# A fused attention and two-layer MoE kernel on one core: its work buffers in two shared pools, the low halves of the softmax weights in two operations, and a new order

## The chip, the core and the metric

The kernel runs on one core of a Trainium2 chip. A core has TensorE (matmuls, PE in the rows, its weight loads PEld), VectorE (DVE), ScalarE (ACT), GpSimd (POOL) and SyncE (SP), which here issues all transfers. Each has a queue of its own and works through it in order. The metric is the time of one execution in microseconds on the device; lower is better.

## The reference

```python
def _attn_ref(q, k, v):            # q, k, v: 4 x 8 x 576 x 64
    scores = scale * np.matmul(q, k.transpose(0, 1, 3, 2))
    kth = np.partition(scores, -top_k, axis=-1)[..., -top_k:-top_k + 1]   # top_k = 32
    scores = np.where(scores >= kth, scores, -1000000000.0)
    scores = scores - np.max(scores, axis=-1, keepdims=True)
    attn = np.exp(scores)
    attn = attn / (np.sum(attn, axis=-1, keepdims=True) + 1e-09)
    return np.matmul(attn, v).astype(np.float32)

def _moe_ref(x, w_in, w_out):      # 2304 tokens, 512 -> 2048 -> 512
    h = x @ w_in
    g = h * (1.0 / (1.0 + np.exp(-1.702 * h)))
    return (g @ w_out).astype(np.float32)

def _moe2_ref(x, w1, w2, w3, w_out):   # 512 -> 1024 twice, product, 1024 -> 1024 -> 512
    return (((x @ w1) * (x @ w2) @ w3) @ w_out).astype(np.float32)
```

The output of the attention, as 2304 tokens of 512, goes through `_moe_ref` and then `_moe2_ref`.

## The kernel before

**Tiles.** The 2304 tokens are 18 tiles of 128. A tile has eight heads, so there are 144 heads of 128 rows and 576 columns; head 48, counted from 0, is the first of the seventh tile. A head goes like this: TensorE makes the scores in one of two score buffers `s_ps` (L997). VectorE finds the 32 largest of each row by four MAX8 (L1019) with a MATCH_REPLACE8 between them (L1022), which writes the scores without the eight just found to `wsb`. ScalarE cuts (L1037) and takes the exponential to `ysb` (L1040), which frees the score buffer. A high half in 16 bits is made of it (ScalarE L1046, GpSimd L1097 or VectorE L1094), then a low half, the rest that the high half misses: 64 columns (L1049) and 512 (L1050), on GpSimd. A DMA transposes both halves to `ats` (L1053), and TensorE multiplies them with the values (L1065).

**Products of two halves.** All large products are made of such pairs: high by high, high by low and low by high, three matmuls of 512 columns (L733 to L735). So the queries, keys, values and every intermediate result of the two MoE layers are scaled, rounded to a high half and have a low half taken from the rest. `split_op` does this for inputs (L404, L421 or L407 the high half; L414 on VectorE, or L417 or L424 with L418 or L427, the low half on GpSimd). The weights come as 64-bit numbers and are taken apart (L477 to L501) and split (L586 to L615) in the first 220 us, beside the first heads.

**The order.** Every step is recorded as an operation with a list of engines that could do it. `PLAN`, a packed table of numbers, gives each its rank and its engine, and `Order.run` issues the operations by rank. It also hands out buffers: a pool is a list of free slots, and an operation that acquires one gets the slot that came free first by the planner's own costs. On the chip the operation waits by semaphores for those that used the slot before it. So the table fixes the order of every engine and the neighbours in each buffer, and a wait in the queue of an engine holds up all that stands behind it.

**Buffers.** Each kind has its own pool: `w` 2 and `y` 3 of 2304 bytes a partition, `hl` 3 (the two halves of a head); `t` 4, `x2t` 1, `h` 3, `f` 3, `stg` 1 of 2 KB (transposed halves, halves, 32-bit intermediate results, loaded inputs).

Of the kernel before, what the change touches and what calls it, by code (L numbers as in the profile page):

```python
# [37 lines left out]
class Order:  # L38
# [17 lines left out]

    def op(self, alts, due, deps=(), env=None, acq=(), rel=(), tag="", lat=None, data=0.6, after=None):
# [4 lines left out]
        o.acq = [(a, env, a) if isinstance(a, str) else a for a in acq]  # L62
        o.rel = [(a, env, a) if isinstance(a, str) else a for a in rel]
# [5 lines left out]
    def run(self, log=None):  # L69
        free = dict.fromkeys("TVAGD", 0.0)  # L70
        lock = moved = 0.0
        for o in sorted(self.ops, key=lambda o: o.rank):
            e, cost, fn, _ = o.alts[0]
            if e == "N":
                o.eng = e
                o.start = o.end = max([0.0] + [d.end + self.GAP[d.eng] for d in o.deps])
                for name, env, key in o.acq:
                    env[key] = None
                continue
# [4 lines left out]
            for name, env, key in o.acq:  # L84
# [16 lines left out]
            for name, env, key in o.rel:  # L101
                if env[key] is not None:
                    self.pools[name].append((o.end + self.GAP[e], o.seq, env[key]))
# [51 lines left out]
    'Z88NeBX2;BpS<7}a;fA{9-3o4++sJJi+b6b8Y<qV-JH(E%6YN~fm6)sS8au^qu)A!uyVPCh?siYP2i?P!k5@k9o{jCN%u)s_GnARi0p*zTSb3>@QNH>8'
# [94 lines left out]
def kernel(  # L250
# [96 lines left out]
    def each(t, n):  # L347
        return [t[:, i] for i in range(n)]
# [1093 lines left out]
```

## Time and profile before

| | |
|---|---|
| median of 3 runs | 1024.83 us (1024.53 to 1025.07) |
| the profiled execution | 1027.73 us, its span 1026.0 us |
| mean granted clock of TensorE | 0.976 |
| TensorE busy, of the span | 947.2 us, 92% |
| VectorE busy | 925.1 us, 90% |
| GpSimd busy | 818.0 us, 80% |
| ScalarE busy | 793.9 us, 77% |

The span is from the first to the last instruction; the execution's own time has what lies around it. Matmuls overlap in time, so TensorE's busy share says that something was running, not that it ran at its peak. The engines have different limits at different times, so the shares are read by stretch of the span.

### The profile page before, as it was taken

The numbers are of one execution on the slowest core, as the hardware profiler recorded it, in microseconds if no ns is written. First come the engines' busy times: TensorE is split into PE (matmuls) and PEld (weight loads), VectorE is DVE, ScalarE is ACT, GpSimd is POOL, SyncE is SP. The second block draws the span as 40 slices with busy tenths as digits, with TensorE's granted clock in tenths as the row PEclk, the third lists the DMA queues.
The fourth block names the chain that finished last, engine by engine and source line by source line (L and its number), as shares of the span: only waits on it lengthen the run. The fifth ranks groups of instructions, "written<-read, shape, count | busy, mean of one in ns | idle before, by whom it ended". The sixth has DMA issues, their size and how long they took to land.

```text
span 1026.0 us, 18847 instructions
## 1 busy us (share of the span) xinstructions
PE 947.2 (92%) x5975; PEld 499.4 (49%) x5975; DVE 925.1 (90%) x2017; ACT 793.9 (77%) x1509; POOL 818.0 (80%) x1195
## 2 busy tenths in 40 slices
PE   4488987889999989999999999999999999999998
PEld 2255554444444544555545554555455545555543
DVE  4998998999999999999999999999999999998543
ACT  7887889977777878888988987878786887667432
POOL 3688788988889988998889998898788878768311
PEclk9689997999999999999999999999999999999999
DMA  8989777877586858688697786678667757545401
GB/s 271 273 274 333 252 171 172 181 160 115 104 140 111 156 98 166 132 144 151 122 164 137 132 160 128 125 130 163 122 130 132 140 103 128 107 89 111 83 1 42
DMA packets 401028, 150.09 MB, mean 146 GB/s; under 512 B 378912, under 2 KB 387104, under 8 KB 400928
## 3 DMA queue, kind: packets, MB, share of 16 engines
q1 hardware_dynamic: 400928, 148.89, 70.1%
q8 instruction: 47, 0.77, 0.3%
q14 instruction: 53, 0.43, 0.1%
HBM read 52.43 MB, written 4.72 MB: 56 GB/s over the span
## 4 chain that ended last, share of the span: by engine, by line
PE 45%; DVE 14%; POOL 13%; ACT 10%; DMA 7%; issue 4%; SPq 0%; POOLq 0%; ACTq 0%; DVEq 0%
PE mm L733 12%; PE mm L734 12%; PE mm L735 12%; DVE m8s L1019 6%; DVE wsb L1022 5%; PE s_ps L997 4%; PE mm L1065 3%; DMA tsb<-hsb 3%; POOL hlb L1050 2%; POOL fsb L1235 2%; DMA stg<-in_q_dram 2%; ACT ysb L1040 2%; POOL hsb L1197 1%; POOL hsb L418 1%; ACT s_ps L1037 1%
## 5 line engine op out<-in xcount | busy, mean ns | idle before, releaser
L1019 DVE MAX8 m8s<-wsb 128x8 f32<-128x576 f32 x432 | 322.3, 753 | 5.6
L1022 DVE MATCH_REPLACE8 wsb<-m8s,wsb 128x576 f32<-128x576 f32 x288 | 213.8, 742 | 0.0
L733 PE MATMUL mm<-w,tsb 128*128 128x512 f16 x432 | 164.5, 381 | 6.9 <-DMA tsb<-hsb 3.6
L735 PEld LDWEIGHTS <-tsb 128*128 128x128 f16 x1072 | 105.0, 98 | 129.3 <-issue 1.9
L733 PEld LDWEIGHTS <-tsb 128*128 128x128 f16 x1072 | 105.0, 98 | 125.4 <-DMA tsb<-hsb 11.5
L1050 POOL TENSOR_TENSOR hlb<-ysb,hlb 128x512 f16<-128x512 f32 x143 | 165.6, 1158 | 0.0
L734 PE MATMUL mm<-w,tsb 128*128 128x512 f16 x432 | 164.2, 380 | 0.0
L735 PE MATMUL mm<-w,tsb 128*128 128x512 f16 x432 | 164.0, 380 | 0.0
L734 PEld LDWEIGHTS <-tsb 128*128 128x128 f16 x1072 | 105.2, 98 | 113.2 <-issue 8.1
L1037 ACT ACTIVATE s_ps<-s_ps,m8s 128x576 f32<-128x576 f32 x144 | 102.4, 711 | 55.2 <-DVE m8s L1019 54.5
L733 PE MATMUL mm<-wout,tsb 128*128 128x512 f16 x344 | 130.8, 380 | 3.4 <-DVE wout L501 1.7
L1040 ACT ACTIVATE ysb<-s_ps,nbs,asm 128x576 f32<-128x576 f32 x144 | 119.8, 832 | 15.2 <-POOL nbs L1029 4.4
L735 PE MATMUL mm<-wout,tsb 128*128 128x512 f16 x344 | 130.6, 380 | 0.9 <-ACT tsb L678 0.9
L734 PE MATMUL mm<-wout,tsb 128*128 128x512 f16 x344 | 130.6, 380 | 0.0
L1019 DVE MAX8 m8s<-s_ps 128x8 f32<-128x576 f32 x144 | 108.9, 757 | 15.2 <-PE s_ps L997 11.2
L733 PE MATMUL mm<-win,tsb 128*128 128x512 f16 x296 | 113.0, 382 | 2.6 <-DMA tsb<-hsb 2.6
L735 PE MATMUL mm<-win,tsb 128*128 128x512 f16 x296 | 112.7, 381 | 0.0
L734 PE MATMUL mm<-win,tsb 128*128 128x512 f16 x296 | 112.7, 381 | 0.0
L997 PE MATMUL s_ps<-kts,qts 128*128 128x288 f16 (+1 forms) x640 | 97.8, 292 | 14.8 <-ACT ysb L1040 11.6
L1022 DVE MATCH_REPLACE8 wsb<-m8s,s_ps 128x576 f32<-128x576 f32 x144 | 107.6, 747 | 0.0
L1235 POOL TENSOR_TENSOR fsb<-fsb 128x512 f32<-128x512 f32 x68 | 86.9, 1278 | 7.7 <-ACT fsb L1232 4.8
L1197 POOL TENSOR_TENSOR hsb<-fsb,hsb 128x512 f16<-128x512 f32 x68 | 78.8, 1158 | 16.5 <-ACT hsb L1191 11.8
(309 smaller groups left out, 1849.9 us busy)
## 6 DMA issues: line engine op xcount, KB each, us to landing
w<-in_moe_w_out_dram SPq DMA_DIRECT2D x24, 512.0 KB, 4.5
w<-in_moe_w_dram SPq DMA_DIRECT2D x22, 512.0 KB, 5.4
w<-in_moe_w_in_dram SPq DMA_DIRECT2D x16, 512.0 KB, 5.4
qts<-qts SPq DMA_DIRECT2D x36, 128.0 KB, 2.5
out_dram<-fsb SPq DMA_DIRECT2D x18, 256.0 KB, 2.4
stg<-in_q_dram SPq DMA_DIRECT2D x15, 256.0 KB, 3.3
stg<-in_v_dram SPq DMA_DIRECT2D x12, 256.0 KB, 2.9
stg<-in_k_dram SPq DMA_DIRECT2D x12, 256.0 KB, 2.9
```

Source lines behind the costliest of these rows:

```text
L733: nc.tensor.matmul(o, a[:, i, :], hi, start=(first and i == 0), stop=False)
L734: nc.tensor.matmul(o, a[:, i, :], lo, start=False, stop=False)
L735: nc.tensor.matmul(o, a[:, 4 + i, :], hi, start=False, stop=(last and i == 3))
L997: nc.tensor.matmul(E["sp"][r : r + n, i], qe[q_][:, h, r : r + n], kt[:, j, i * HS : (i + 1) * HS], start=k_ == 0, stop=k_ == 1,)
L1019: nc.vector.max(out=E["m8"][:, 8 * i : 8 * i + 8], in_=E["sp"] if i == 0 else E["w"])
L1022: nc.vector.match_replace(out=two(E["w"]) if i == 0 else E["w"], in_to_replace=E["m8"][:, 8 * i : 8 * i + 8], in_values=E["sp"] if i == 0 ...
L1037: nc.scalar.activation(E["sp"], E["sp"], AF.Prelu, bias=E["m8"][:, TOPK - 1 : TOPK], scale=-1.0, alpha=1.0 / FAR)
L1040: nc.scalar.activation(two(E["y"]), E["sp"], AF.Exp, bias=E["nb"], scale=nesc)
L1050: nc.gpsimd.tensor_tensor(hl()[:, S + SR : 2 * S], E["y"][:, 0:SM], hl()[:, 0:SM], op=ALU.subtract)
L1065: nc.tensor.matmul(heads_av()[r : r + n, j_, c0 : P + 1], e["at"][:, i, r : r + n], v2[:, j_, blk, c0 : P + 1], start=(i == 0), stop=(i == 8),
L1197: return lambda: eng.tensor_tensor(E["h"][:, C : 2 * C], src(), E["h"][:, 0:C], op=ALU.subtract)
L1235: nc.gpsimd.tensor_tensor(E["f"], E["f"], E["f2"], op=ALU.mult)
```

## The change

**Two shared pools.** `w`, `y` and `hl` become one pool `y` of eight blocks of 2304 bytes, and `t`, `x2t`, `h`, `f` and `stg` one pool `f` of eleven blocks of 2 KB, seen as 16-bit or transposed halves where needed. A twelfth block (`tsb` 0) joins that pool when the weights no longer need it. The bytes stay the same: 2 + 3 + 3 = 8 and 4 + 1 + 3 + 3 + 1 = 12.

**Low halves in two parts.** The two instructions of a head's low half (L1049, L1050) become two operations, `a lor` and `a lo` (L1061, L1064 of the changed kernel), each with GpSimd or VectorE as its engine. The products of the MoE layers (`g`, `p`) also get their engine from the table.

**The order.** `PLAN` is a new table, made with somewhat other costs.

```diff
+    def share(self, name, pool, view):
+        self.kinds[name] = pool, view
...
-        o.acq = [(a, env, a) if isinstance(a, str) else a for a in acq]
...
+        kind = lambda n: self.kinds.get(n, (n, None))
+        acq = [(a, env, a) if isinstance(a, str) else a for a in acq]
...
+        o.acq = [(kind(n)[0], e, k, kind(n)[1]) for n, e, k in acq]
...
-                env[key] = s[2]
+                env[key] = s[2] if view is None else view(s[2])
+                env["slot", key] = s[2]
...
-    od.pool("w", each(wsb, 2))
-    od.pool("y", each(ysb, 3))
-    od.pool("hl", each(hlb, 3))
...
+    od.pool("y", each(ysb, 8))
+    od.share("w", "y", None)
+    od.share("hl", "y", half)
...
-    od.pool("h", each(hsb, 3))
-    od.pool("f", each(fsb, 3))
+    od.pool("f", each(usb, 11))
+    od.share("stg", "f", None)
+    od.share("h", "f", half)
+    od.share("t", "f", turned_)
+    od.share("x2t", "f", turned_)
...
-        def f_lo():
-            nc.gpsimd.tensor_tensor(hl()[:, S : S + SR], E["y"][:, SM:S], hl()[:, SM:S], op=ALU.subtract)
-            nc.gpsimd.tensor_tensor(hl()[:, S + SR : 2 * S], E["y"][:, 0:SM], hl()[:, 0:SM], op=ALU.subtract)
+        def f_lor(eng):
+            return lambda: eng.tensor_tensor(hl()[:, S : S + SR], E["y"][:, SM:S], hl()[:, SM:S], op=ALU.subtract)
+
+        def f_lo(eng):
+            return lambda: eng.tensor_tensor(hl()[:, S + SR : 2 * S], E["y"][:, 0:SM], hl()[:, 0:SM], op=ALU.subtract)
...
-        los = [("G", 1.42, f_lo, 0.0)]
-        if t == NTILE - 1:
-            los.append(("V", 0.85, od.two(f_lo_v), 0.0))
-        lo = op(los, due + 7, deps=[hi], env=E, rel=["y"], tag="a lo")
+        lor = op(
+            [("G", 0.31, f_lor(nc.gpsimd), 0.0), ("V", 0.14, od.two(f_lor(nc.vector)), 0.0)], due + 7, deps=[hi], env=E, tag="a lor"
+        )
+        los = [("G", 1.13, f_lo(nc.gpsimd), 0.0), ("V", 0.68, od.two(f_lo(nc.vector)), 0.0)]
+        lo = op(los, due + 7, deps=[hi, lor], env=E, rel=["y"], tag="a lo")
```

Most lines of the changed kernel stand 10 to 15 further down: L404 to L427 are L414 to L437 there, L477 to L501 are L487 to L511, L672 is L682, L1019 and L1022 are L1031 and L1034, L1029 is L1041.

VectorE before, in the program's first heads, where the fourth pair of heads of the first batch is prepared (`win` holds its keys, `kr` the remainder):

```order
L414 SCALAR_TENSOR_TENSOR kr_88<-rest,kvc,kr_88 64x2x64
L672 TENSOR_SCALAR tsb<-mm_101 128x512
L1029 TENSOR_SCALAR nbs<-m8s,asm 128x1
L914 RECIPROCAL kvc<-mm_99 128x1
L974 RECIPROCAL asm<-asm 128x1
L916 COPY kvinv<-mm_99 128x1
L1022 MATCH_REPLACE wsb<-m8s,wsb 128x576
L414 SCALAR_TENSOR_TENSOR hsb<-win,kvc,hsb 128x4x64 x2
L681 TENSOR_SCALAR tsb<-mm_101 128x512
L501 SCALAR_TENSOR_TENSOR win<-mm_100,win 128x512
L672 TENSOR_SCALAR tsb<-mm_102 128x512
```

VectorE of the changed kernel at the same place (`ysb` takes what `wsb` took, `usb` what `tsb` and `hsb` took):

```order
L424 SCALAR_TENSOR_TENSOR kr_84<-rest,kvc,kr_84 64x2x64
L1031 MAX m8s<-ysb 128x8 x2
L1041 TENSOR_SCALAR nbs<-m8s,asm 128x1
L926 RECIPROCAL kvc<-mm_96 128x1
L986 RECIPROCAL asm<-asm 128x1
L682 TENSOR_SCALAR usb<-mm_95 128x512
L682 TENSOR_SCALAR usb<-mm_98 128x512
L511 SCALAR_TENSOR_TENSOR win<-mm_96,win 128x512
L1034 MATCH_REPLACE ysb<-m8s,ysb 128x576
L1031 MAX m8s<-s_ps_94 128x8
L1034 MATCH_REPLACE ysb<-m8s,s_ps_94 128x576
```

The low half of the keys (`hsb<-win`, two instructions) is no longer on VectorE.

GpSimd before at this place, where it makes the high half of those keys (L421) between steps of the weights:

```order
L427 TENSOR_TENSOR hsb<-wout,hsb 128x8x64
L569 TENSOR_SCALAR tsb<-ident,wsm 128x128
L509 TENSOR_SCALAR win<-w_72 128x512
L421 TENSOR_SCALAR hsb<-win,kvc 128x8x64
L509 TENSOR_SCALAR win<-w_72 128x512
L487 TENSOR_SCALAR win<-w_72 128x512
L1097 TENSOR_SCALAR hlb<-ysb 128x576
L1011 TENSOR_SCALAR asm<-kvinv,asm 128x1
```

GpSimd of the changed kernel there:

```order
L1026 TENSOR_SCALAR asm<-asm 128x1
L519 TENSOR_SCALAR win<-w_72 128x512
L497 TENSOR_SCALAR win<-w_72 128x512
L431 TENSOR_SCALAR usb<-win,kvc 128x8x64
L427 TENSOR_SCALAR wout<-wout,kvc 128x512
L428 TENSOR_TENSOR usb<-wout,usb 128x8x64
L427 TENSOR_SCALAR usb<-usb,asm 128x512
L428 TENSOR_TENSOR usb<-usb 128x8x64
L427 TENSOR_SCALAR win<-win,kvc 128x512
L428 TENSOR_TENSOR usb<-win,usb 128x8x64
L519 TENSOR_SCALAR win<-w_72 128x512
```

The low halves of keys and queries (L427 and L428, two instructions each) now stand on GpSimd, three pairs in a row ahead of the next step of the weights.

GpSimd before, a little later, with the low halves of two heads (`hlb<-ysb`):

```order
L592 TENSOR_SCALAR win<-w_73,wsm 128x512
L1049 TENSOR_TENSOR hlb<-ysb,hlb 128x64
L1050 TENSOR_TENSOR hlb<-ysb,hlb 128x512
L569 TENSOR_SCALAR tsb<-ident,wsm 128x128
L592 TENSOR_SCALAR w_73<-wout,wsm 128x512 x2
L509 TENSOR_SCALAR wout<-w_72 128x512
L1029 TENSOR_SCALAR nbs<-m8s,asm 128x1
L1049 TENSOR_TENSOR hlb<-ysb,hlb 128x64
L1050 TENSOR_TENSOR hlb<-ysb,hlb 128x512
```

GpSimd of the changed kernel there (`ysb<-ysb`):

```order
L579 TENSOR_SCALAR tsb<-ident,wsm 128x128
L1061 TENSOR_TENSOR ysb<-ysb 128x64
L427 TENSOR_SCALAR usb<-usb,kvc 128x512
L428 TENSOR_TENSOR v2s<-usb,v2s 128x2x4x64
L1064 TENSOR_TENSOR ysb<-ysb 128x512
L602 TENSOR_SCALAR w_73<-wout,wsm 128x512
L579 TENSOR_SCALAR tsb<-ident,wsm 128x128
L1111 TENSOR_SCALAR ysb<-ysb 128x576
L1061 TENSOR_TENSOR ysb<-ysb 128x64
```

The 64 columns (L1061) and the 512 (L1064) of a head now stand apart, with the split of a value between them.

## Rows read from the trace of the kernel before

**Rows 1.** Busy us of each engine by stretch (windows), all engines.

```profile
core 0: us, PE busy (x) PEld busy (x) DVE busy (x) ACT busy (x) POOL busy (x), PEclk, DMA share, GB/s
0.00:150.00 150.00, 108.23 (x654) 65.11 (x655) 127.90 (x280) 122.00 (x231) 109.10 (x169) 0.91 0.91 264
150.00:200.00 50.00, 41.69 (x279) 23.94 (x278) 47.25 (x110) 47.60 (x91) 45.27 (x71) 0.83 0.80 175
200.00:400.00 200.00, 182.39 (x1199) 93.33 (x1196) 191.47 (x427) 158.64 (x304) 171.41 (x257) 0.99 0.71 132
400.00:950.00 550.00, 543.09 (x3428) 281.43 (x3429) 524.63 (x1142) 441.75 (x841) 476.00 (x678) 1.00 0.71 131
950.00:1026.00 76.00, 71.80 (x420) 35.59 (x418) 33.87 (x62) 23.88 (x46) 16.17 (x24) 0.99 0.21 40
```

**Rows 2.** Timeline of TensorE at 850 us: start us, us, instruction.

```profile
850.10 0.38 PE L735 MATMUL mm<-w,tsb 128*128 128x512 f16 x1
850.32 0.38 PE L733 MATMUL mm<-wout,tsb 128*128 128x512 f16 x1
```

**Rows 3.** Waits: who waited for whom, us in total, times, longest.

```profile
PE s_ps L997 <- ACT ysb L1040: 11.6, 19, 2.0
...
DVE m8s L1019 <- PE s_ps L997: 11.2, 20, 1.3
```

**Rows 4.** Groups by line: line, engine, operation, tiles | busy us, mean ns.

```profile
L1019 DVE MAX8 m8s<-wsb 128x8 f32<-128x576 f32 x432 | 322.3, 753 | 5.6
L1022 DVE MATCH_REPLACE8 wsb<-m8s,wsb 128x576 f32<-128x576 f32 x288 | 213.8, 742 | 0.0
```

**Rows 5.** Line L1019 (ns min/median/max, first and last start); timeline of VectorE.

```profile
L1019 DVE MAX8 m8s<-s_ps x144: 739/756/768, 30.5 to 947.1; 128x8 f32<-128x576 f32 x144
L1019 DVEq EVENT_SEMAPHORE  x115: 21/21/50, 102.9 to 947.0; - x115
...
387.61 0.75 DVE L1019 MAX8 m8s<-s_ps 128x8 f32<-128x576 f32 x1
```

**Rows 6.** Line L414: ns min/median/max, first and last start.

```profile
L414 DVE SCALAR_TENSOR_TENSOR kr<-rest,kvc,kr x6: 333/336/443, 13.1 to 733.9; 64x128 f16<-64x128 f32 x6
...
L414 DVE SCALAR_TENSOR_TENSOR v2s<-rest,kvc,v2s x6: 334/750/1218, 15.6 to 762.8; 128x128 f16<-128x128 f32 x6
...
L414 DVE SCALAR_TENSOR_TENSOR hsb<-win,kvc,hsb x2: 485/704/924, 54.3 to 54.7; 128x256 f16<-128x256 f32 x2
...
L414 DVE SCALAR_TENSOR_TENSOR v2s<-stg,kvc,v2s x2: 472/556/639, 362.4 to 362.7; 128x256 f16<-128x256 f32 x2
```

**Rows 7.** Groups by line and shape, VectorE: count | busy us, mean ns.

```profile
L407 DVE TENSOR_SCALAR hsb<-w,kvc 128x512 f16<-128x512 f32 x1 | 0.5, 515 | 0.0
...
L407 DVE TENSOR_SCALAR v2s<-rest,kvc 128x128 f16<-128x128 f32 x1 | 0.4, 397 | 0.0
...
L672 DVE TENSOR_SCALAR tsb<-mm 128x512 f16<-128x512 f32 x4 | 2.7, 683 | 0.5 <-PE mm L904 0.5
...
L1029 DVE TENSOR_SCALAR nbs<-m8s,asm 128x1 f32<-128x1 f32 x55 | 14.4, 261 | 0.3
...
L1102 DVE TENSOR_TENSOR hlb<-ysb,hlb 128x64 f16<-128x64 f32 x1 | 0.2, 205 | 0.0
...
L1094 DVE CAST hlb<-ysb 128x576 f16<-128x576 f32 x3 | 1.9, 640 | 0.0
```

**Rows 8.** Groups by line and shape, ScalarE and GpSimd.

```profile
L1046 ACT CAST hlb<-ysb 128x576 f16<-128x576 f32 x97 | 64.5, 670 | 3.0 <-DMA ats<-hlb 1.9
...
L424 ACT ACTIVATE stg<-stg,kvc 128x512 f32<-128x512 f32 x8 | 5.8, 722 | 0.1
...
L1050 POOL TENSOR_TENSOR hlb<-ysb,hlb 128x512 f16<-128x512 f32 x143 | 165.6, 1158 | 0.0
```

**Rows 9.** Waits of ScalarE for a block: the first and last of eight.

```profile
ACT hsb L1191 <- DMA tsb<-hsb: 4.0, 3, 2.4
...
ACT fsb L1327 <- POOL fsb L1235: 1.0, 2, 0.8
```

**Rows 10.** DMA issues: kind, count, median us from issue to landing.

```profile
ats<-hlb SPq DMA_TRANSPOSE x142, 3.4
```

More of the change, by code (lines that the diff above doesn't have):

```diff
@@ L46, in __init__ @@
         self.pools = {}
+        self.kinds = {}
         self.both = set()
@@ L76, in run @@
                 o.start = o.end = max([0.0] + [d.end + self.GAP[d.eng] for d in o.deps])
-                for name, env, key in o.acq:
+                for name, env, key, view in o.acq:
                     env[key] = None
@@ L102, in run @@
                 if env[key] is not None:
-                    self.pools[name].append((o.end + self.GAP[e], o.seq, env[key]))
+                    self.pools[name].append((o.end + self.GAP[e], o.seq, env.get(("slot", key), env[key])))
+                    env[key] = None
             if log is not None:
@@ L235 @@
+    '8|Y$szz2V=n3~kdkVzIdkT4qR4rPyn5TrNq^Go}lqbnk#*^$R=P4gw!Bf$b=qVeY5})R&<f$B=;mPz=^;Glx4+9X#Mg'
 )
@@ L314 @@
     qts = mem([P, 3, H, P], F16, "qts")
-    wsb = mem([P, 2, S], F32, "wsb")
-    ysb = mem([P, 3, S], F32, "ysb")
-    hlb = mem([P, 3, 2 * S], F16, "hlb")
+    ysb = mem([P, 8, S], F32, "ysb")
     ats = mem([P, 2, 9, P], F16, "ats")
     xsb = mem([P, H, D + 1], F32, "xsb")
-    tsb = mem([P, 7, C], F32, "tsb")
-    hsb = mem([P, 3, 2 * C], F16, "hsb")
-    fsb = mem([P, 3, C], F32, "fsb")
+    usb = mem([P, 11, C], F32, "usb")
+    tsb = mem([P, 3, C], F32, "tsb")
     psb = mem([P, 2, C], F32, "psb")
-    stg = mem([P, 1, C], F32, "stg")
     rest = mem([P, 2, 2, D], F32, "rest")
@@ L352 @@
     od.pool("q", each(qts, 3))
-    od.pool("w", each(wsb, 2))
-    od.pool("y", each(ysb, 3))
-    od.pool("hl", each(hlb, 3))
+    half = lambda z: z.bitcast(F16)
+    turned_ = lambda z: z.bitcast(F16).rearrange("p (k m) -> p k m", k=8)
+    od.pool("y", each(ysb, 8))
+    od.share("w", "y", None)
+    od.share("hl", "y", half)
     od.pool("at", each(ats, 2))
     od.pool("x", [xsb])
-    od.pool("t", [tsb[:, i, :].bitcast(F16).rearrange("p (k m) -> p k m", k=8) for i in range(4)])
-    od.pool("x2t", [tsb[:, 4, :].bitcast(F16).rearrange("p (k m) -> p k m", k=8)])
-    od.pool("pt", [tsb[:, i, :].bitcast(F16).rearrange("p (k m) -> p k m", k=8) for i in (5, 6)])
-    od.pool("h", each(hsb, 3))
-    od.pool("f", each(fsb, 3))
+    od.pool("f", each(usb, 11))
[3 more added lines that the diff above has]
+    od.share("x2t", "f", turned_)
+    od.pool("pt", [turned_(tsb[:, i, :]) for i in (1, 2)])
     od.pool("p", each(psb, 2))
-    od.pool("stg", each(stg, 1))
     od.pool("blk", [block(w, i) for w, n0, n in ((win, 0, 16), (wout, 0, 16), (w34, 0, 8), (w12, 2 * NRAW, 16)) for i in range(n0, n)])
```

281 lines of the change are left out of this document (144 added, 137 removed).

## Prediction

> **What bounds the kernel now.** I first read the busy times by stretch [rows 1]. From 400 to 950 us TensorE is busy 543.09 of 550 us, and its large matmuls follow each other at 0.21 us, one behind the other [rows 2]. From there to the end the work goes at TensorE's own pace: only what TensorE has done by about 400 us can still move the end. Before that it is not full: 108.23 of 150, 41.69 of 50 and 182.39 of 200 us, so 67.7 of the first 400 us are idle. The reader is to see who is full in that part: VectorE with 127.90, 47.25 and 191.47 us, 366.6 of 400, while ScalarE has 122.00, 47.60 and 158.64 (328.2) and GpSimd 109.10, 45.27 and 171.41 (325.8). One stretch is different: from 150 to 200 us ScalarE is the fullest of the three.
>
> Then I read the waits [rows 3]. VectorE waits for TensorE's scores 20 times, 11.2 us in the whole program, and TensorE for a free score buffer 19 times, 11.6 us. Both are small: in the first 400 us the kernel is held by the amount of VectorE work ahead of TensorE's, not by one late transfer. The selection of the 32 largest makes up most of it: 144 heads with four MAX8 of 0.753 us and three MATCH_REPLACE8 of about 0.742 us [rows 4], 5.2 us a head. The first head starts at 30.5 us, the last at 947.1 [rows 5], one in 916.6/143 = 6.4 us.
>
> **The change part by part.** The two listings hold the same 144 heads, the same products and the same matmuls but one pair, and TensorE's order is nearly the same: ahead of the score matmuls of any one head its work differs by some matmuls at most. So I price what moves between the other engines ahead of head 48. Its selection starts at 387.61 us [rows 5], about where TensorE becomes full.
>
> What VectorE loses ahead of head 48, counted in the two listings: of the low halves at L414 three of 128x128 (0.732 us mean), two `hsb<-win` of 128x256 (0.704), two `v2s<-stg` (0.556) and two of 64x128 (0.354), together 2.20 + 1.41 + 1.11 + 0.71 = 5.43 us [rows 6]; two at L407 (0.515 + 0.397 = 0.91); two at L672 (2 x 0.683 = 1.37); five small ones at L1029 (5 x 0.261 = 1.31) [rows 7]. That is 9.02 us; one at L589 goes as well and one of the same size at L602 comes, which I set against each other. What it gains: one L772, a high half that the trace has on ScalarE alone (between nothing, if it only fills a wait, and the 0.68 of L672, which reads a PSUM bank in the same way; I take 0.68), one new remainder of 64 columns (0.21, L1102), one CAST and one COPY that only stand earlier (at most 0.64 each, L1094: 1.28) [rows 7]. An instruction with more than one wait carries an EVENT_SEMAPHORE ahead of it, 21 ns at the median [rows 5]; there are 17 more such waits ahead of head 48, 0.36 us, and 76 in the program. Together 2.53 us. Net: 9.02 - 2.53 = 6.5 us less work on VectorE where it bounds.
>
> What the means of [rows 6] hold must be asked. The same instruction at L414 takes 334 ns at the least and 1218 at the most for 128x128, while the smaller one is steady at 333 to 443. So part of the mean is time in which it was held, not work. The Trainium skill (SBUF — State Buffer, section "Who interferes with whom") says that VectorE and GpSimd share one pair of ports, that a VectorE instruction with two SBUF inputs contends with a GpSimd one that reads SBUF, and that the second to come is blocked until the first is done; the spread of L414 agrees. By that rule this change has a cost: the work goes to GpSimd, which then holds the ports for longer. With the shortest durations of [rows 6] (3 x 0.334, 2 x 0.485, 2 x 0.472, 2 x 0.333) the 5.43 us are 3.6, and the net is 4.7. I take 6.5, since a held VectorE does nothing else either, and keep 4.7 as the low end; without the two that only stand earlier it is 7.8, the high end.
>
> Where it goes: ahead of head 48 ScalarE gets ten more casts at L1046 (0.670 us), five more scalings at L424 (0.722) and loses a few, about 10 us more in all by these rows [rows 8]; GpSimd gets the low halves and loses ten casts, about 3 us more. In the first 400 us ScalarE idles 71.8 and GpSimd 74.2 us, which covers both, except from 150 to 200 us, where ScalarE has 2.4 us free. In the listing about 2.4 us of its additions fall between heads 8 and 16, that is in this stretch. If ScalarE and VectorE take turns in being late there, some of it shows: between nothing and 2.4 us; I take 0.9.
>
> The low halves of the softmax weights are two operations now, but still two instructions (L1049, L1050 before), 138 and 143 of them on GpSimd. GpSimd does the same work; at seven places a part is on VectorE, six remainders of 0.21 and one block that was there before. Nothing for the end: after 400 us VectorE sets nothing (524.63 of 550), and if it did, six times 0.21 is 1.3 us.
>
> The shared blocks. Seven kinds of buffer become two pools of the same bytes. What this gives is a release that is not waited for. On ScalarE the trace has eight rows in which it waits for a block, from 4.0 us (for a transpose to read the old halves) to 1.0, in sum 14.9 [rows 9]. ScalarE is not the bound, so I price this at nothing; the other bound is in the rivals. What it costs is a wait that was not there: before, VectorE's first MATCH_REPLACE8 of a head wrote to one of two buffers that only VectorE used. In the changed program 88 of 144 also wait for another engine, 64 of them for a DMA queue (the transpose that read the weights of an earlier head) and 44 for GpSimd. Behind such an instruction stands all of VectorE. Eight blocks serve three uses. By the rows of one operation each, a head holds one block for the selection (5.2 us alone, about twice that when two heads alternate), one from the exponential to the low half (0.67 + 1.16 and the exponential, estimated at 3) and one from the cast to the landing of the transpose (0.67 + 1.16 + 3.4 = 5.2 us) [rows 4, 8, 10]: 13.4 to 18.6 us of block time in 6.4 us, so two to three of eight blocks are in use. The other five are handed out three in 6.4 us, so a block rests for about ten. I price the wait at nothing, and the late case as a rival.
>
> Sum: -6.5 + 0.9 = -5.6 us. The profiled execution took 1027.73 us with a span of 1026.0; the median of the runs is 1024.83, and I carry the difference over: **1024.83 - 5.6 = 1019.2 us**, -0.55%.
>
> **The rivals.** Under 0.2% (2 us) a measurement of this kernel can hardly tell from no change.
>
> A. As forecast. VectorE's relief reaches TensorE before 400 us. From 4.7 - 2.4 = 2.3 us to 7.8 us of gain: 1017 to 1022.5.
>
> B. More than that: the blocks were in the way. The Trainium skill (Perfetto Trace Analysis, section "Optimization Strategy") says that bubbles that repeat on the engine that should be full can mean too few buffers for the next tile. As a mechanism here: the 14.9 us of [rows 9] were handed to TensorE. If they lie evenly, 400/1026 of them come before 400 us, 5.8 us, and the time is 1013.4. For it: TensorE's 67.7 idle us leave room. Against: no wait for a block stands among the large ones, and those that do are on an engine with room.
>
> C. No change. ScalarE and GpSimd are given 13 us ahead of head 48, and each of their results is waited for by someone. If the exponential comes as much later as the selection comes earlier, TensorE gets its work at the old times: 1024.8. For it: ScalarE is the fullest engine from 150 to 200 us. Against: both have over 70 us free.
>
> D. Slower: VectorE waits for blocks. Place: the first MATCH_REPLACE8 of each head. If one in five of the 88 finds its block 0.8 us late (a transpose lands 3.4 us after its issue at the median, and queues behind others), that is 14 us on VectorE, and with A's gain taken off the time is 1033. It decides from 5.6 us of such lateness on, if that falls before 400 us; after it, TensorE's backlog covers some. Against it: the rest of about ten us that a block has.
>
> **How the numbers follow.** A 0.46, B 0.15, C 0.19, D 0.20. Faster by over 0.2% are A but for a little at its edge, and B: 0.61; within 0.2%, C: 0.19; slower, D: 0.20. The likeliest is A, 1019.2, with its own range of 1017 to 1022.5. The range for 8 in 10 reaches from below B's 1013.4, with the ends of A's terms added, to most of D: 1010 to 1030.
>
> **What would show it.** Right: VectorE's busy time in the first 400 us holds 6 to 7 us less of what is listed above; TensorE's in the first 400 rises by 5 to 8; from 400 us it is as full as before (99% of its stretch); the first MATCH_REPLACE8 shows no waits worth naming. A is wrong if VectorE's idle time in the first 400 us grows by what its work falls; C if ScalarE's wait rows swell at 150 to 200 us; D if a wait for `ats<-ysb` or a GpSimd low half stands ahead of MATCH_REPLACE8. B shows as the rows of [rows 9] gone and TensorE's rise over 10 us. The whole is wrong if TensorE is not full after 400 us.

## The result and the profile after

The changed kernel takes 1012.46 us (1010.88 to 1013.42, 4 runs) against 1024.68: a ratio of 0.9879, interval 0.9862 to 0.9896. A second group of runs gave 0.9873 (0.9856 to 0.9890). The prediction was 1019.2 us, a gain of 5.6; the gain is about 12.5 us, at the value of rival B (1013.4), which had a chance of 0.15. The time lies inside the stated range of 1010 to 1030, but the gain is more than twice the forecast one.

The same stretches as [rows 1], from the trace of the changed kernel (busy us of each engine):

```profile
core 0: us, PE busy (x) PEld busy (x) DVE busy (x) ACT busy (x) POOL busy (x), PEclk, DMA share, GB/s
0.00:150.00 150.00, 109.54 (x694) 66.68 (x695) 128.29 (x279) 130.47 (x248) 111.89 (x179) 0.87 0.95 269
150.00:200.00 50.00, 38.89 (x261) 21.47 (x261) 49.18 (x113) 49.17 (x94) 48.24 (x72) 0.91 0.86 185
200.00:400.00 200.00, 188.90 (x1235) 96.67 (x1233) 192.46 (x427) 165.19 (x318) 175.31 (x267) 0.99 0.71 132
400.00:950.00 550.00, 547.02 (x3461) 283.68 (x3459) 522.10 (x1137) 432.35 (x817) 472.06 (x685) 1.00 0.72 132
950.00:1012.00 62.00, 57.81 (x329) 28.36 (x327) 23.27 (x42) 18.18 (x35) 14.92 (x19) 0.98 0.08 22
```

TensorE has 337.33 us in the first 400 (109.54 + 38.89 + 188.90) where it had 332.31. That is 5.0 more, as the prediction wanted (5 to 8). But from 400 to 950 us it also has 547.02 where it had 543.09, and there the prediction saw nothing to gain. Of rival B's two signs one came: ScalarE's waits of [rows 9] are gone but for 0.4 us. The other, a rise of TensorE by over 10 us, did not come: it is 5.0. Three rows of the waits (in total, times, longest), two of which answer to [rows 3]:

```profile
DVE m8s L1031 <- PE s_ps L1009: 11.2, 22, 1.5
...
PE s_ps L1009 <- ACT ysb L1052: 7.4, 17, 1.0
...
ACT ysb L1052 <- POOL nbs L1041: 4.9, 11, 1.5
```

TensorE waits 7.4 instead of 11.6 us for a score buffer. VectorE's groups with the first MATCH_REPLACE8 of a head, which now takes a shared block, the load ahead of it, and the small scalings (count | busy us, mean ns | idle before it):

```profile
L1034 DVE MATCH_REPLACE8 ysb<-m8s,s_ps 128x576 f32<-128x576 f32 x144 | 107.6, 747 | 0.0
...
L1034 DVE MATCH_VALUE_LOAD ysb<-m8s,s_ps 128x8 f32 x144 | 11.5, 80 | 1.5
...
L1041 DVE TENSOR_SCALAR nbs<-m8s,asm 128x1 f32<-128x1 f32 x40 | 10.4, 261 | 0.3
```

The same load in the kernel before:

```profile
L1022 DVE MATCH_VALUE_LOAD wsb<-m8s,s_ps 128x8 f32 x144 | 11.7, 81 | 1.3
```

The idle time before all 144 first MATCH_REPLACE8 is 0.0, and before the short load ahead of each 1.5 us in the whole program, 1.3 before: rival D does not happen. The scalings on VectorE are 40, where [rows 7] has 55.

**Where the time went.** It is better to divide the span by the work done than by fixed times: up to the MAX8 that starts head 48, and on to that of head 120. Here are these two stretches before, in the columns of [rows 1]:

```profile
0.00:387.61 387.61, 321.06 (x2048) 176.21 (x2049) 354.40 (x789) 316.60 (x603) 315.21 (x483) 0.94 0.79 188
387.61:805.35 417.74, 410.37 (x2635) 213.19 (x2634) 401.16 (x883) 349.06 (x674) 370.92 (x533) 1.00 0.75 139
```

and in the changed kernel:

```profile
0.00:378.30 378.30, 316.50 (x2043) 173.67 (x2044) 348.64 (x773) 324.92 (x617) 314.52 (x489) 0.93 0.82 192
378.30:792.10 413.80, 410.52 (x2639) 213.43 (x2638) 397.87 (x872) 349.27 (x674) 375.68 (x552) 1.00 0.76 139
```

Read VectorE's busy time (third pair of numbers) against the length of the stretch. To head 48 the time falls by 9.3 us: 5.8 of VectorE's work (354.40 to 348.64) and 3.5 of its idle time (33.2 to 29.7). From there to head 120 it falls by 3.9 more: 3.3 of work (401.16 to 397.87) and 0.6 of idle time. After head 120, 1.2 are left. The sum is the 14.4 us between the two spans; some two of these belong to the profiled execution of before, which took 1027.73 us where the medians of the kernel before lie between 1024.68 and 1026.16. Each row is a single execution. A second one of the changed kernel (after_again) reads, to head 48:

```profile
0.00:377.30 377.30, 316.89 (x2044) 172.62 (x2045) 347.18 (x773) 324.99 (x617) 314.57 (x489) 0.95 0.81 193
```

Its work is 7.2 us less than before and its idle time 3.1 (30.1). So differences of one or two microseconds between two such rows are not safe.

So the term that the prediction worked out, 6.5 us of VectorE work ahead of head 48, is there with 5.8 to 7.2. What it did not have are VectorE's idle time and everything after 400 us.

### The profile page after: what moved, and what is told of

It reads as the page before. It is cut to its first block, busy times and chain, and to the rows that moved or that the text cites. A ratio compares the mean times of both kernels' runs of the same rounds, so it can differ in the third digit from the quotient of the medians.

```text
span 1011.6 us, 18848 instructions
## 1 busy us (share of the span) xinstructions
PE 942.2 (93%) x5973; PEld 496.9 (49%) x5973; DVE 915.3 (90%) x1995; ACT 795.3 (79%) x1508; POOL 822.4 (81%) x1220
## 4 chain that ended last, share of the span: by engine, by line
PE 56%; DVE 3%; POOL 3%; DMA 2%; ACT 2%; issue 1%; SPq 0%; POOLq 0%; DVEq 0%; ACTq 0%
PE mm L743 16%; PE mm L745 15%; PE mm L744 15%; PE s_ps L1009 5%; PE mm L1079 4%; DVE m8s L1031 1%; DVE ysb L1034 1%; DMA usb<-usb 1%; POOL ysb L1064 1%; DMA ats<-ysb 0%; DMA tsb<-tsb 0%; PE mm L708 0%; DMA usb<-tsb 0%; POOL usb L1207 0%; POOL usb L1245 0%
## 5 line engine op out<-in xcount | busy, mean ns | idle before, releaser
L1031 DVE MAX8 m8s<-ysb 128x8 f32<-128x576 f32 x432 | 321.8, 753 | 5.2
L1034 DVE MATCH_REPLACE8 ysb<-m8s,ysb 128x576 f32<-128x576 f32 x288 | 213.8, 742 | 0.0
L1064 POOL TENSOR_TENSOR ysb<-ysb 128x512 f16<-128x512 f32 x143 | 165.5, 1159 | 0.4
L743 PE MATMUL mm<-w,usb 128*128 128x512 f16 x373 | 141.6, 380 | 4.3 <-DMA usb<-usb 3.3
L1049 ACT ACTIVATE s_ps<-s_ps,m8s 128x576 f32<-128x576 f32 x144 | 102.3, 711 | 51.1 <-DVE m8s L1031 48.0
L745 PE MATMUL mm<-w,usb 128*128 128x512 f16 x373 | 141.6, 380 | 0.0
L744 PE MATMUL mm<-w,usb 128*128 128x512 f16 x373 | 141.4, 379 | 0.0
L745 PEld LDWEIGHTS <-usb 128*128 128x128 f16 x876 | 86.0, 98 | 104.6 <-issue 1.9
L743 PEld LDWEIGHTS <-usb 128*128 128x128 f16 x876 | 85.8, 98 | 99.1 <-DMA usb<-usb 6.5
L744 PEld LDWEIGHTS <-usb 128*128 128x128 f16 x876 | 86.0, 98 | 91.1 <-issue 5.5
L1052 ACT ACTIVATE ysb<-s_ps,nbs,asm 128x576 f32<-128x576 f32 x144 | 119.6, 830 | 12.5 <-POOL nbs L1041 4.9
L1031 DVE MAX8 m8s<-s_ps 128x8 f32<-128x576 f32 x144 | 108.8, 755 | 13.5 <-PE s_ps L1009 11.2
L1034 DVE MATCH_REPLACE8 ysb<-m8s,s_ps 128x576 f32<-128x576 f32 x144 | 107.6, 747 | 0.0
L743 PE MATMUL mm<-wout,usb 128*128 128x512 f16 x273 | 104.3, 382 | 1.8 <-DVE usb L691 0.6
L744 PE MATMUL mm<-wout,usb 128*128 128x512 f16 x273 | 104.2, 382 | 0.0
L745 PE MATMUL mm<-wout,usb 128*128 128x512 f16 x273 | 104.0, 381 | 0.0
L743 PE MATMUL mm<-win,usb 128*128 128x512 f16 x230 | 88.3, 384 | 2.1 <-DVE w L511 1.1
L744 PE MATMUL mm<-win,usb 128*128 128x512 f16 x230 | 88.0, 383 | 0.0
L745 PE MATMUL mm<-win,usb 128*128 128x512 f16 x230 | 87.9, 382 | 0.0
L1079 PEld LDWEIGHTS <-ats 128*128 128x128 f16 (+1 forms) x1440 | 73.8, 101 | 19.6 <-issue 7.1
L1009 PEld LDWEIGHTS <-qts 128*128 128x128 f16 (+1 forms) x640 | 55.9, 101 | 53.3 <-issue 24.8
```

What stands on the lines that cost most here:

```text
L743: nc.tensor.matmul(o, a[:, i, :], hi, start=(first and i == 0), stop=False)
L744: nc.tensor.matmul(o, a[:, i, :], lo, start=False, stop=False)
L745: nc.tensor.matmul(o, a[:, 4 + i, :], hi, start=False, stop=(last and i == 3))
L1009: nc.tensor.matmul(E["sp"][r : r + n, i], qe[q_][:, h, r : r + n], kt[:, j, i * HS : (i + 1) * HS], start=k_ == 0, stop=k_ == 1,)
L1031: nc.vector.max(out=E["m8"][:, 8 * i : 8 * i + 8], in_=E["sp"] if i == 0 else E["w"])
L1034: nc.vector.match_replace(out=two(E["w"]) if i == 0 else E["w"], in_to_replace=E["m8"][:, 8 * i : 8 * i + 8], in_values=E["sp"] if i == 0 ...
```

## Experiments

Every kernel was timed against the kernel before on the same chip. To compare, ratios are turned to us with 1025.5 us, about the median of before: the changed kernel (0.9876, the mean of its two groups) stands at -12.7. The half interval of each ratio is 0.0010 to 0.0020, 1 to 2 us, so that a difference of two kernels under 2 us says little. The expectations reckon from single groups of runs, so the prices that they name differ from those below by up to a microsecond. Names with b_ are made from the kernel before, those with a_ from the changed one.

### The pools alone

**b_pools**, the kernel before with its order and engines, and the two pools:

```diff
-    wsb = mem([P, 2, S], F32, "wsb")
-    ysb = mem([P, 3, S], F32, "ysb")
-    hlb = mem([P, 3, 2 * S], F16, "hlb")
+    ysb = mem([P, 8, S], F32, "ysb")
...
+    od.pool("y", each(ysb, 8))
+    od.share("w", "y", None)
+    od.share("hl", "y", half)
...
+    od.pool("f", each(usb, 11))
+    od.share("stg", "f", None)
+    od.share("h", "f", half)
+    od.share("t", "f", turned_)
```

> The kernel before with its own order and engines; only its buffers are shared: the selection, exponential and weight-halves buffers become one pool of eight blocks, the turned operands, feed-forward halves, feed-forward values and staging another of eleven (the one buffer of the second layer's transpose stays apart). If shared blocks by themselves gave the gain (rival B and the 14.9 us of waits of ScalarE for a block), 1019 or less and those waits gone. If the gain is VectorE's lighter work, 1023 to 1026. If blocks that VectorE must wait for are the price (rival D), 1027 or more.

1022.37 us, ratio 0.9970 (0.9957 to 0.9983): -3.1 us, between the first two cases. **b_pools_f** has the pool of eleven only.

> The kernel before with its own order and engines; only the pool of eleven is shared (turned operands, feed-forward halves and values, staging), the selection's buffers stay apart. The 14.9 us of ScalarE's waits for a block are all of this pool: if they made the gain of 3.1 us of b_pools, 1021 to 1023 and the waits gone; if the selection's pool did, 1024 to 1026.

1023.98 us, ratio 0.9974 (0.9964 to 0.9984): -2.7 us. By this the pool of eleven does most of it, though the 0.4 us between the two kernels is within the noise. ScalarE's waits there (us in total, times, longest):

```profile
ACT usb L1200 <- POOL usb L1244: 11.3, 11, 2.5
...
ACT hlb L1055 <- DMA ats<-hlb: 1.4, 2, 0.8
...
ACT usb L1389 <- DMA ats<-hlb: 0.6, 1, 0.6
...
ACT usb L1351 <- DMA tsb<-usb: 0.6, 1, 0.6
...
ACT usb L413 <- DMA ats<-hlb: 0.4, 1, 0.4
```

The first row is a wait for data (the product that the cast then reads) and stays (9.4 us before). Of the 14.9 us of [rows 9], 1.9 are waits for the block of a head's two halves (`hlb`), which is not in this pool; 1.4 of these are still there (second row). Of the other 13.0, 0.6 + 0.6 + 0.4 = 1.6 are left. So the pool takes away 11.4 us of ScalarE's waits for a block, and the kernel gains 2.7. Most of the freed time became other waits of ScalarE: its idle time in the whole span falls from 232.1 to 227.6 us only, and its wait for the product with the values (`xsb`) grows from 14.8 to 19.9. Sharing blocks thus gives 3 us where rival B had 5.8. That the gain comes through these waits is likely but not shown by itself: the loads, too, no longer share one staging block, and ScalarE's wait for loaded queries falls from 9.5 to 8.1 us. In b_pools it is VectorE that comes sooner:

```profile
0.00:384.91 384.91, 321.49 (x2048) 176.15 (x2049) 353.49 (x788) 316.24 (x603) 314.57 (x483) 0.95 0.79 189
```

Against the kernel before, head 48 starts 2.7 us sooner; VectorE's work differs by 0.9, the rest is idle time (31.4 instead of 33.2).

### What work costs on each engine

In each of these, one instruction is done twice at some heads.

```diff
-            nc.vector.max(out=E["m8"][:, 8 * i : 8 * i + 8], in_=E["sp"] if i == 0 else E["w"])
+            for _ in range(2 if i == 0 and 8 * t + h in range(2, 42, 5) else 1):
+                nc.vector.max(out=E["m8"][:, 8 * i : 8 * i + 8], in_=E["sp"] if i == 0 else E["w"])
```

This is **a_dup_early**, and **b_dup_early** in the kernel before; **a_dup_late** has range(60, 100, 5). **a_gdup** and **b_gdup** double the 512-column low half on GpSimd (L1064, L1050 before) at heads 0, 1, 2, 11 and 41, **a_adup** the cast on ScalarE (L1058) at nine heads.

> The changed kernel with the first MAX8 of eight heads (2, 7, ... 37, at 60 to 320 us) done twice: 6.0 us more VectorE work ahead of head 48; the output is the same. If VectorE's work ahead of head 48 is paid in full, as the prediction has it, 1018.5. If early and late work cost the same (the late one cost 4.4 us for the same 6.0), 1017. If another engine holds the early stretch, 1013 to 1015.

> The changed kernel with the first MAX8 of eight heads (60, 65, ... 95, at 450 to 650 us) done twice: 8 x 0.755 = 6.0 us more VectorE work where TensorE is 99% busy; the output is the same. By the reading of the prediction (from 400 us TensorE alone sets the pace) no change, 1012.5. If VectorE bounds there as well, 4 to 6 us more: 1016.5 to 1018.5.

> The kernel before with the first MAX8 of heads 2, 7, ... 37 done twice: 6.0 us more VectorE work ahead of head 48. If VectorE's work has the same price in the old order as in the new one (a_dup_early: 5.5 of 6.0), 1030 to 1032. If in the old order another engine holds the early stretch, which would explain why the low halves do not pay there, 1026 to 1028.

> The kernel before with the 512-column low half of heads 0, 1, 2, 11 and 41 done twice on GpSimd: 5.8 us more GpSimd work about where the low halves of keys and values were put. If in the old order GpSimd's load there is paid for (it eats what VectorE saves in b_lows), 1028 to 1031. If GpSimd has room there, 1025 to 1026.5, and the low halves fail for the place of their first few.

> The same doubling in the changed kernel (5.8 us more GpSimd work at heads 0, 1, 2, 11 and 41). If the new order gives GpSimd the room that the old one lacks, 1013 to 1014.5 against 1013.4. If GpSimd's load costs the same in both, 1015 to 1019.

> The changed kernel with ScalarE's cast of the softmax weights done twice at nine heads (2, 8, 13, 18, 23, 27, 32, 37, 41): 9 x 0.67 = 6.0 us more ScalarE work ahead of head 48; the output is the same. The same amount cost 5.5 us on VectorE and 3.8 on GpSimd. If idle time is room, ScalarE (53 us idle up to head 48, GpSimd 64) pays as GpSimd does, 3 to 4.5 us: 1016 to 1018. If ScalarE's idle time covers it, 1013 to 1014.5.

| kernel | us | ratio (interval) | work added | time added |
|---|---|---|---|---|
| a_dup_early | 1019.11 | 0.9933 (0.9920 to 0.9945) | VectorE, ahead of head 48, 6.0 | 5.8 |
| b_dup_early | 1031.71 | 1.0055 (1.0039 to 1.0072) | the same | 5.6 |
| a_dup_late | 1016.85 | 0.9912 (0.9896 to 0.9928) | VectorE, heads 60 to 95, 6.0 | 3.7 |
| a_gdup | 1017.21 | 0.9917 (0.9901 to 0.9933) | GpSimd, ahead of head 48, 5.8 | 4.2 |
| b_gdup | 1029.04 | 1.0031 (1.0019 to 1.0043) | the same | 3.2 |
| a_adup | 1015.53 | 0.9897 (0.9880 to 0.9913) | ScalarE, ahead of head 48, 6.0 | 2.2 |

(Time added: the ratio less 0.9876, or less 1 for the two of before, times 1025.5.) The intervals leave each of these some 2 us either way. VectorE's work ahead of head 48 is paid nearly in full, in both orders: the mechanism of rival A, the forecast, holds. Two things of the prediction do not. Late VectorE work is paid at 3.7 of 6.0 us, although TensorE is 99% busy there. And GpSimd is not free: 64 us of idle time up to head 48 do not hide 5.8 us. ScalarE's 2.2 us (with 53 us idle) stand at the edge of the noise. Where GpSimd's cost appears is seen in a_gdup:

```profile
0.00:381.42 381.42, 319.09 (x2043) 174.14 (x2044) 348.20 (x773) 325.15 (x617) 320.33 (x494) 0.95 0.82 191
```

VectorE has 348.2 us of work, as in the changed kernel (348.64), but 33.2 us of idle time where that has 29.7 and 30.1 in its two traces: head 48 starts 3 to 4 us later because VectorE waits.

The way by which late work counts stands in TensorE's waits from 400 to 950 us, in the kernel before and in the changed one:

```profile
PE s_ps L997 <- ACT ysb L1040: 2.9, 6, 0.9
```

```profile
PE s_ps L1009 <- ACT ysb L1052: 0.2, 1, 0.2
```

A score buffer is free when the exponential has read it, and the exponential waits for VectorE's selection. In six places TensorE had to wait for that; now in one. With the late work of a_dup_late it is four again:

```profile
PE s_ps L1009 <- ACT ysb L1053: 1.4, 4, 0.5
```

TensorE's idle time in this stretch is 4.7 us there (545.28 of 550 busy) and 3.0 in the changed kernel, so these waits show the way but not all of the 3.7 us.

### The engines alone, and undone

**b_engines** takes the kernel before and gives the low halves of keys and values and the scalings (nbs) the engines that the change gives them; **a_engines_back** does the reverse in the changed kernel. Pools and order stay. With the low halves go the scalings ahead of some of them: in b_lows, ScalarE has five more of these and GpSimd six.

```diff
+ALT = {
+    17: 0, 38: 0, 46: 2, 47: 2, 56: 2, 57: 2, 70: 0, 77: 0, 78: 0, 88: 1, 89: 1, 91: 0,
...
+}
...
-        o.alts = alts if k is None else [alts[k]]
+        o.alts = alts if k is None else [alts[ALT.get(len(self.ops), k)]]
```

(The table holds an operation's number and which of its alternatives runs; these lines are those of a_engines_back.) The others are parts of it: **b_lows** and **a_lows_back** the low halves without the scalings, **b_lows_early** and **b_lows_late** those ahead of head 48 and those behind head 10, **b_pools_lows** b_pools and b_lows together.

> The kernel before with its own order and buffers; only the low halves of keys and values and the small scalings that form the bias of the exponential run on the engines that the change gives them (13 low-half instructions and 15 scalings leave VectorE in all, nine and five of them ahead of head 48). If VectorE's work is the price, 6.7 us less of it ahead of head 48 gives about 1018, and up to 11.7 us less in all gives 1013 if VectorE also bounds after 400 us. If order or buffers matter, within 2 us of 1024.7.

> The changed kernel with its own order and buffers; the same low halves and scalings go back to the engines of the kernel before. If VectorE's work is the price: 6.7 us more of it ahead of head 48 gives 1019, and 11.7 us more in all gives 1024 if VectorE bounds after 400 us too. If order and buffers made the gain: 1012 to 1014.

> The kernel before with its own order and buffers; only the low halves of keys and values move to GpSimd (13 instructions off VectorE), the scalings stay. If the scalings on GpSimd, late in its queue, made the 33 us of b_engines: 1019 to 1026 here. If the low halves on GpSimd held its queue: 1040 or more.

> The changed kernel; only the low halves of keys and values go back to VectorE (13 instructions, nine ahead of head 48, 5.4 us there and 7 to 8 us in all). If VectorE's work is the price, 1017 to 1020 (most of the 8.5 us of a_engines_back); if the scalings carried that loss, 1012 to 1014.

> The kernel before with its own order and buffers; only those low halves of keys and values that stand ahead of head 48 move to GpSimd (nine instructions, 5.4 us off VectorE). If these pay and the four later ones cost (in the profile of b_lows, heads gained 4 us up to head 100 and lost it again after), 1021 to 1023. If the early ones do not pay in this order either, 1025 to 1028.

> The kernel before with only those low halves of keys and values on GpSimd that stand behind head 10 (those in the stage that builds the weights stay on VectorE). b_lows gave +1.9, the part ahead of head 48 alone +2.9. If the move fails in the old order because of the stage that builds the weights, where GpSimd makes the low bits that others wait for, 1022 to 1024.5 here. If it fails everywhere, 1026 or more.

> The kernel before in its own order, with both shared pools and with the low halves of keys and values on GpSimd. Alone, the pools gave -3.1 us and the low halves +1.9. If those only add, 1024 to 1025. If it is the shared blocks that let the move pay (a low half on GpSimd holds its staging block longer, and before there is one such block), 1016 to 1019. If it needs the new order, 1022 or more.

| kernel | us | ratio (interval) | against its base, us |
|---|---|---|---|
| b_engines | 1058.23 | 1.0319 (1.0300 to 1.0339) | +32.7 |
| b_lows | 1027.66 | 1.0019 (1.0009 to 1.0030) | +1.9 |
| b_lows_early | 1028.57 | 1.0028 (1.0017 to 1.0039) | +2.9 |
| b_lows_late | 1027.42 | 1.0015 (1.0003 to 1.0028) | +1.5 |
| b_pools_lows | 1024.97 | 0.9989 (0.9980 to 0.9999) | -1.1 |
| a_engines_back | 1020.95 | 0.9955 (0.9940 to 0.9971) | +8.1 |
| a_lows_back | 1019.98 | 0.9939 (0.9927 to 0.9952) | +6.5 |

In the new order the low halves on GpSimd are worth 6.5 us; in the old one the same move costs 1.9. I had expected 1013 to 1018 of b_engines, or no change within 2 us if order or buffers matter, and 1019 to 1026 or at least 1040 of b_lows; none of these came. No kernel made from the old order gained from the move: neither the early nor the late ones alone do, and with the pools the two effects only add (-3.1 + 1.9 = -1.2, measured -1.1), so it is not the blocks either.

VectorE's rows up to head 48 (and, for b_lows, on to head 120) say how the gain is lost. In b_lows, in b_pools_lows and in a_lows_back:

```profile
0.00:383.91 383.91, 320.71 (x2047) 174.08 (x2048) 348.89 (x780) 317.11 (x604) 321.29 (x496) 0.95 0.80 190
383.91:803.92 420.01, 412.07 (x2636) 213.62 (x2635) 400.31 (x880) 351.65 (x678) 370.90 (x537) 1.00 0.74 138
```

```profile
0.00:387.83 387.83, 321.26 (x2048) 175.42 (x2049) 349.11 (x779) 317.67 (x604) 321.37 (x496) 0.95 0.80 188
```

```profile
0.00:383.88 383.88, 320.10 (x2042) 175.89 (x2043) 351.61 (x783) 324.27 (x615) 308.44 (x476) 0.94 0.81 190
```

To head 48, VectorE has as little work in b_lows as in the changed kernel (348.89 us, 348.64 there), but it idles 35.0 us instead of 29.7. With the second row, up to head 120, its work is 6.4 us less than before and its idle time 4.9 more (54.7 instead of 49.8); what is left of the gain, 1.4 us, is no more than the two by which the profiled execution of before was long. In b_pools_lows it has 349.11 us of work to head 48 and idles 38.7, where b_pools has 353.49 and 31.4: 4.4 less work, 7.3 more idle time. What is taken off VectorE comes back as VectorE waiting. In the old order that fits the price of GpSimd: b_lows has GpSimd at 321.29 us instead of 315.21, 6.1 more, and b_gdup paid 3.2 for 5.8. The changed kernel has that work too, and GpSimd still only 314.52, because other work went elsewhere (ScalarE 324.92 instead of 316.60).

But a_lows_back does not fit it. There VectorE gets 3.0 us of work over the changed kernel and GpSimd loses 6.1 (308.44), and yet VectorE idles no less: 32.3 us, where the changed kernel has 29.7 and 30.1. Neither b_lows nor a_lows_back has an order made for its engines. So part of the 6.5 us may be the price of that misfit and not the worth of the move; no run here parts the two.

The 33 us of b_engines are another wait. ScalarE, TensorE and VectorE there:

```profile
DVE m8s L1030 <- PE s_ps L1008: 33.1, 33, 5.1
...
ACT ysb L1051 <- POOL nbs L1040: 30.9, 25, 4.0
...
PE s_ps L1008 <- ACT ysb L1051: 30.6, 28, 4.4
```

and the row of the kernel before for the second of these:

```profile
ACT ysb L1040 <- POOL nbs L1029: 4.4, 8, 1.1
```

The longest of these waits, in the timelines of GpSimd and then ScalarE (start us, us, instruction, idle before it and its cause):

```profile
426.25 1.27 POOL L1341 TENSOR_TENSOR psb<-psb,fsb 128x512 f32<-128x512 f32 x1
427.50 0.37 POOL L428 TENSOR_SCALAR rest<-rest,kvc 128x128 f32<-128x128 f32 x1
427.96 0.42 POOL L429 TENSOR_TENSOR v2s<-rest,v2s 128x128 f16<-128x128 f32 x1
428.34 0.30 POOL L1060 TENSOR_TENSOR hlb<-ysb,hlb 128x64 f16<-128x64 f32 x1
428.60 1.15 POOL L1061 TENSOR_TENSOR hlb<-ysb,hlb 128x512 f16<-128x512 f32 x1
429.74 0.36 POOL L1040 TENSOR_SCALAR nbs<-m8s,asm 128x1 f32<-128x1 f32 x1
```

```profile
425.42 0.71 ACT L1048 ACTIVATE s_ps<-s_ps,m8s 128x576 f32<-128x576 f32 x1
430.14 0.83 ACT L1051 ACTIVATE ysb<-s_ps,nbs,asm 128x576 f32<-128x576 f32 x1 [4.00 <-POOL nbs L1040]
```

ScalarE is done with the cut (L1048) at 426.1 us and needs the bias for the exponential (L1051). VectorE has the selection by then (the cut needed it), but the scaling (L1040) stands in GpSimd's queue behind five others, and GpSimd is never idle: it comes at 429.74, and ScalarE has waited 4.00 us. So in the old order the scalings come late, the exponential waits for them (30.9 instead of 4.4 us), holds the score buffer (TensorE waits 30.6 us for it instead of 11.6), and VectorE waits for the scores (33.1 instead of 11.2). In the changed kernel 104 scalings are on GpSimd instead of 89, and the exponential waits 4.9 us for them.

### The split of the low halves, and the kernel again

**a_lor_one** puts the two parts of each head's low half on one engine again (seven remainders); **after_again** is the changed kernel.

```diff
+ALT = {1254: 0, 3814: 0, 3829: 0, 5058: 0, 5091: 0, 5260: 0, 5344: 1}
```

> The changed kernel with the two parts of each head's low half on one engine again (seven remainders of 64 columns change engine). The prediction priced the split at nothing: 1011 to 1014, as after_again. If the split matters, 1014 or more.

> The changed kernel itself once more, as the base for the others of this group: 1011 to 1014, a ratio of 0.988 to the kernel before.

1013.34 us, 0.9880 (0.9862 to 0.9899), against 1013.41, 0.9873 (0.9856 to 0.9890), on the same chip. Which engine has the seven remainders changes nothing that can be measured. The two parts still stand apart in the order there, so the split itself was not undone. No kernel tried is faster than the changed one by more than the noise.

## Why the prediction was wrong

**Right.** The relief of VectorE ahead of head 48: 6.5 us forecast, 5.8 in the profile (7.2 in that of after_again, 347.18 us), and such work is paid at 5.8 of 6.0 us. TensorE's busy time to 400 us rises by 5.0. The first MATCH_REPLACE8 does not wait for its block. The engines of the split low halves cost and give nothing. Of the two sums, the one with the mean durations (6.5) is nearer than the one with the shortest (4.7). But that the time in which the instructions were held went with them is not shown: with nine of them back on VectorE (a_lows_back) it has 3.0 to 4.4 us more work up to head 48, where the means make 5.43 and the shortest durations 3.6. The rule on the shared ports (the Trainium skill, SBUF — State Buffer, section "Who interferes with whom") had named such holding. Whether the price of GpSimd's work comes through the ports or through late results, no run here tells apart.

**The step that failed: "only what TensorE has done by about 400 us can still move the end".** It was read from a busy share of 99%, and the sign set for it, TensorE as full as before from 400 us, came true all the same. But a_dup_late pays 3.7 of 6.0 us, and the trace has TensorE waiting for score buffers after 400 us in six places. VectorE is 96% busy from head 48 to 120, which fits the two taking turns. The change removes 3.3 us of VectorE work from head 48 to 120, and that stretch is 3.9 us shorter; at the price of a_dup_late that work is worth 2.0. Not all of the 3.9 need be this work: in b_pools the stretch is 3.0 us shorter with only 1.1 us less of it. The listings showed that more VectorE work goes after head 48; I left it out of the sum.

**A second step: the blocks were priced "at nothing" because ScalarE "is not the bound".** They give 3.1 us (b_pools), and VectorE's idle time falls there (33.2 to 31.4 us up to head 48); by which wait this reaches VectorE is not shown. Rival B had named the blocks; shared evenly over the span, its 14.9 us were 5.8, of which about half was paid. That the whole change came out at B's 1013.4 us is luck: shared blocks alone give 3.1 of the 12.7. The rule of the Trainium skill behind it (Perfetto Trace Analysis, section "Optimization Strategy": bubbles that repeat on the engine that should be full can mean too few buffers) agrees with b_pools in its result, -3.1 us; the waits stood on ScalarE, though, which is not the fullest engine, so a reader should look for them on every engine.

**A third: idle time as room.** "In the first 400 us ScalarE idles 71.8 and GpSimd 74.2 us, which covers both", with 0.9 us allowed for one stretch. It does not: 5.8 us more on GpSimd cost 4.2 and 3.2, and 6.0 on ScalarE some 2.2. (The work itself came out as 8.3 us more on ScalarE up to head 48, where the prediction had about 10, and 0.7 less on GpSimd, where it had about 3 more.) By these prices the low halves on GpSimd (5.5 us off VectorE, 6.1 more on GpSimd in b_lows) would have been forecast at a gain of 1 to 2 us. This error is on the other side, and hid part of the first two.

**What makes up the gain.** Of 12.7 us, the pools alone give 3.1. The changed kernel without the moves of low halves and scalings is at -4.6 (a_engines_back), so order and the remaining moves add 1.5 to the pools, within what can be measured, and the moves in the new order 8.1. The last two cannot be parted: in the old order the same moves lose 32.7, and the new order was made for them, so that a_engines_back may lose something by the misfit alone. Nor do the prices measured here add up to the gain: as an estimate, 5.8 us of early VectorE work at 5.8 of 6.0 give 5.6, 3.3 us of late work at 3.7 of 6.0 give 2.0, the pools 3.1, and 8.3 us more on ScalarE at 2.2 of 6.0 cost 3.0, together 7.7. Some 5 of the 12.7 us have no price here. That they come from the order is argued from b_engines and b_lows, which lose where the changed kernel gains; it is not shown by itself. The prediction priced the moves from the list of instructions and took the order as given.

**Open:** the cause of those 5 us, and which places in the new order make the moves pay. The new order holds up to four blocks at once for exponentials and four for their halves, where the separate pools had three of each, so the new order with the old buffers was not tried; and no single placement was moved by itself.

## What to carry to other kernels

When three engines feed a fourth in one order, a busy share of 99% on the fourth does not end the account: look for waits on its inputs and double a small instruction on each feeder to learn its price, before idle time is taken as room. Count what is taken off the bounding engine, then ask what its idle time will be: here, of 6.4 us taken off VectorE up to head 120, 4.9 came back as waiting in the old order, and none in the new. A reassignment of engines belongs to an order made for it; tried alone, or undone alone, it does not tell what the pair is worth.

## What the runs showed of the hardware that I had not expected

Two things. First, how a queue that is worked through in order multiplies a small change: b_engines differs from b_lows only in the scalings, 34 of 0.37 us put on GpSimd and 19 taken off, 5.6 us net, and the time went from +1.9 to +32.7 us, since behind the wait of one stood the exponential, the score buffer and the next head.

Second, up to head 48 TensorE's busy time fell from 321.06 to 316.50 us with nearly the same matmuls (2048 and 2043 in the records). In b_pools, which is faster than before too, it was 321.49, so the lower busy time is not needed for a gain. A higher clock does not explain it: from 150 to 200 us the granted clock was 0.91 instead of 0.83, but in the first 150 us 0.87 instead of 0.91, and over the whole way to head 48 0.93 and 0.95 in the two traces of the changed kernel, where before has 0.94. Nothing here was made to test it, and the cause is open.
